# One visit instead of two: key sums of a whole batch in one slot, numerators of two head pairs in one slot, in blocks 2 to 6 of a fused attention and mixture-of-experts kernel

## The chip, the core and the metric

The kernel runs on one core of a Trainium2 chip. The core has five engines with instruction streams of their own: TensorE (PE, matrix products into the PSUM memory; its weight loads are listed as PEld), VectorE (DVE), ScalarE (ACT), GpSimd (POOL) and SyncE (SP). Here POOL and SP mainly issue DMA transfers. The metric is the device time of one launch in microseconds, the median of three runs.

## The reference

Linear attention with cosine and sine weights, then a layer of eight experts whose mixing weights are balanced by eight Sinkhorn rounds.

```python
q_p = phi(q, cos_w, sin_w)          # relu(q)*cos and relu(q)*sin side by side: 64 -> 128 features
k_p = phi(k, cos_w, sin_w)
kv  = einsum('bhsf,bhsd->bhfd', k_p, v)
z   = sum(k_p, axis=2)
num = einsum('bhsf,bhfd->bhsd', q_p, kv)
den = einsum('bhsf,bhf->bhs', q_p, z)[..., None] + 1e-06
x   = num / den                     # 8 batches, 8 heads, 576 tokens, 64 wide -> x is 4608 x 512
...
P = exp(x @ w_gate - max); 8 rounds of dividing P by its row sums and by its column sums
out = sum over the 8 experts e of P[:, e] * (relu(x @ w1[e]) @ w2[e])
```

## The kernel before

The kernel has two stages. In the first, the attention of one batch after another is laid in between the matrix products of expert 0. In the second, experts 1 to 7 run over all tokens. The change touches the first stage alone.

**Blocks and slots.** The first stage is a loop over blocks j = 0 to 6. A block is expert 0 over 512 tokens, in 16 slots. Slots 0 to 7 are the first product (ffn1): four matmuls of 512 columns into an h_ps bank, and a relu by ScalarE into hT. Slots 8 to 15 are the second product (ffn2): four matmuls of 512 columns into a y_ps bank, and after every second slot a copy by ScalarE into acc. After the matmuls of slot s of block j, the loop runs the functions that the table todo holds for (j, s); at(j, s, fn, ...) puts them there (lines 584 to 728). Functions of one slot run in the order in which at was called.

**Order.** TensorE, VectorE and ScalarE are reached through wrappers (te, ve, se) that tie each instruction to the one written before it on its engine. So the written order is the order in which each engine works, and an instruction that waits holds up all that is written behind it on its engine.

**What block j does besides expert 0.** For batch b = j + 1 it finishes the attention; for batch b + 1 it prepares; of batch b + 2 it loads the inputs. hk counts four head pairs, and a "half" is two of them. The functions are these:

- prep_k (line 339): the relu of a head pair's keys, on ScalarE for these blocks. prep_q (346): on VectorE, the relu and the multiplication with cosine and sine into q_p, one of three buffers; then SP issues a DMA that transposes q_p into one of eight q_pT places (two of them lie in acc_lo and acc_hi, and show under these names). prep_kv (371): on VectorE, the multiplication of the keys into k_p (four buffers) and the copy of the values beside a column of ones.
- sums (443): for one half, 2 head pairs x 9 chunks x 2 heads = 36 matmuls, each 64 rows by 128 columns of weights with 65 streamed columns. The two heads use the upper and the lower 64 rows of the array. The results go to two small_ps banks, from where ScalarE copies kv_sb and VectorE makes zsel.
- denominators (496): 24 matmuls with 32 columns of weights, side by side in three groups of columns; VectorE then adds the epsilon, takes the reciprocal, and splits it in two fp16 parts, hi and hl.
- attend (531), for one head pair: three matmuls of 96 rows and 192 streamed columns spread the reciprocals over the feature rows into two small_ps banks, ScalarE copies them to rb, then four matmuls of 128 rows and 64 columns of weights form the numerators (two of 384 and two of 192 streamed columns, the two heads in the left and the right 64 columns of the array) into two other banks, and VectorE multiplies them with rb into xT, which ffn1 and the gates read.
- gates (563): the logits of the tokens of batch j, and their exponential on ScalarE.
- load (198): six DMAs issued by POOL, held back until the VectorE instruction written just before it is done.

All small results, of sums, denominators, attend and gates, share one ring of four PSUM banks, named small_ps. A bank is used again when its readers are done.

**The slots before.** For j = 3 to 6: sums of the second half in slot 0, denominators in slot 3, gates in slot 5, attend in slots 6, 8, 10 and 12, prep_q in 4, 5, 7 and 9, prep_kv of the next batch in 7, 9, 11 and 13, loads in 11 and 12, and sums of the next batch's first half in slot 14. Block 2 differs from it in some of the prep slots. Block 6 prepares no further batch.

After block 6, two more blocks of expert 0 (j = 7 and 8) run beside the Sinkhorn rounds on VectorE. The rounds begin when gates(7), in slot 0 of block 7, have been exponentiated.

Of the kernel before, what the change touches and what calls it, by code (L numbers as in the profile page):

```python
# [25 lines left out]
def kernel(  # L26
# [19 lines left out]
    C = S // HP  # L46
# [134 lines left out]
    with ExitStack() as p1:  # L181
# [107 lines left out]
        C3 = C // 3  # L289
# [178 lines left out]
        def sums_made(b, half, kv_ps):  # L468
            kv_sb, zsel = kvs[b]
            W_ = D + 1 if b else D  # L470
            for hh in range(2):
                kv_v = kv_ps[hh][:, 0 : 2 * W_].rearrange("p (hk d) -> p hk d", d=W_)
                se.copy(out=kv_sb[:, 2 * half : 2 * half + 2, hh, :], in_=kv_v[:, :, 0:D])
                if b:
                    ve.tensor_tensor(
                        out=zsel[:, 4 * half + hh : 4 * half + 4 : 2, :],
                        in0=zmask[:, 4 * half + hh : 4 * half + 4 : 2, :],
                        in1=kv_v[:, :, D : D + 1].to_broadcast([P, 2, 32]),
                        op=ALU.mult,
                    )  # L480
# [47 lines left out]
            )  # L528
            hls[b] = hl

        def attend(b, hk):

            parts = ((0, 2 * C3), (2 * C3, C))
            rb_ps = [ps_s.tile([P, 512], FP32, name="small_ps") for _ in parts]
            rb = rb_pool.tile([P, C * HP], FP32, name="rb")
            for i, (c0, c1) in enumerate(parts):
                for j in range(c0 // C3, c1 // C3):
                    te.matmul(
                        out=rb_ps[i][:, (j * C3 - c0) * HP : ((j + 1) * C3 - c0) * HP],
                        lhsT=spread[0:96, j, hk].rearrange("p hh d -> p (hh d)"),  # L540
                        rhs=hls[b][:],
                        start=True,
                        stop=True,
                    )
                se.copy(out=rb[:, c0 * HP : c1 * HP], in_=rb_ps[i][:, 0 : (c1 - c0) * HP])
            num_ps = [ps_s.tile([P, 512], FP32, name="small_ps") for _ in parts]
            for i, (c0, c1) in enumerate(parts):
                for hh in range(2):
                    te.matmul(
                        out=num_ps[i][hh * HP : (hh + 1) * HP, 0 : (c1 - c0) * HP],  # L550
                        lhsT=kvs[b][0][:, hk, hh, :],
                        rhs=qTs[b, hk][:, c0:c1, hh * HP : (hh + 1) * HP],
                        start=True,
                        stop=True,
                    )
                ve.tensor_tensor(
                    out=xT[:, hk, b * S + c0 * HP : b * S + c1 * HP],
                    in0=num_ps[i][:, 0 : (c1 - c0) * HP],
                    in1=rb[:, c0 * HP : c1 * HP],
                    op=ALU.mult,  # L560
                )
# [25 lines left out]
        def at(block, slot, fn, *args):  # L587
            todo.setdefault((block, slot), []).append((fn, args))
# [40 lines left out]
        for hk in range(HK):  # L629
            attend(0, hk)  # L630
            for kt in ((), (0,), (1,), (2, 3))[hk]:
                for ft, h_ps in enumerate(first_ps):
                    te.matmul(
                        out=h_ps[:],
                        lhsT=w0[0][:, kt, ft * P : (ft + 1) * P],
                        rhs=xT[:, kt, 0:TCH],
                        start=(kt == 0),
                        stop=(kt == KT - 1),
                    )
                    if kt == KT - 1:  # L640
                        se.activation(out=hT[:, ft, 0:TCH], in_=h_ps[:], func=AF.Relu)
            for i in ((), (0,), (1, 2), ())[hk]:
                prep_k(1, i, i < 2)
            for i in ((), (0,), (1,), (2, 3))[hk]:
                if i == 3:
                    prep_k(1, i, False)
                prep_kp(1, i)
# [3 lines left out]
        for j in range(B):  # L651
            b = j + 1
            if j == 0:

                def sums_first(half):
                    sums_made(1, half, sums_begun(1, half))

                for hk in range(HK):
                    for i in range(3):
                        at(0, (5, 6, 6, 7)[hk], turn, 1, hk, i, i != 1)  # L660
                    if hk == 0:
                        at(0, 5, prep_q, 1, 3)
                    if hk == 2:
                        at(0, 6, prep_v, 1, 0, se.copy)
                        at(0, 6, prep_v, 1, 2, ve.tensor_copy)
                    if hk == 3:
                        at(0, 7, prep_v, 1, 1, se.copy)
                        at(0, 7, prep_v, 1, 3, ve.tensor_copy)
                for half in range(2):
                    at(0, 7, sums_first, half)  # L670
                at(0, 8, denominators, 1)
                at(0, 10, gates, 0)
                for hk in range(HK):
                    at(0, 11 + hk, attend, 1, hk)
            elif b < B:
                if j == 1:
                    at(0, 13, load, b + 1, 0, "q", True)
                    for hk in range(HK):
                        if hk >= 2:
                            at(j, 0, prep_k, b, hk, False)  # L680
                        at(j, 0, prep_kp, b, hk)
                        at(
                            j, (0, 0, 1, 3)[hk], prep_v, b, hk,
                            (ve.tensor_copy, se.copy)[hk // 2],
                        )
                    for name, half in (("q", 1), ("k", 0), ("k", 1), ("v", 0), ("v", 1)):
                        at(j, 0, load, b + 1, half, name, True)
                    at(j, 3, sums, b, 0)
                    at(j, 5, sums, b, 1)
                else:  # L690
                    at(j, 0, sums, b, 1)
                at(j, 6 if j == 1 else 3, denominators, b)
                for hk in range(HK):
                    at(j, (9, 10, 12, 13)[hk] if j == 1 else 6 + 2 * hk, attend, b, hk)
            if j:
                at(j, 5, gates, j)
            if j == 0:
                for half in range(2):
                    at(j, 3, load, b + 1, half)
                for slot, fn, hk, *args in (  # L700
                    (8, prep_q, 0), (11, prep_k, 0), (12, prep_q, 1), (12, prep_k, 1),
                    (13, prep_q, 2), (14, prep_q, 3),
                ):
                    at(j, slot, fn, b + 1, hk, *args)
            elif b + 1 < B:
                for slot, fn, hk in (
                    (4, prep_q, 0), (5, prep_q, 1), (8, prep_k, 0), (8, prep_q, 2),
                    (9, prep_k, 1), (10, prep_kv, 0), (10, prep_k, 2), (12, prep_q, 3),
                    (12, prep_kv, 1), (12, prep_k, 3), (13, prep_kv, 2), (14, prep_kp, 3),
                    (14, prep_v, 3),  # L710
                ) if j == 1 else (
                    (4, prep_q, 0), (5, prep_k, 0), (5, prep_q, 1), (6, prep_k, 1),
                    (7, prep_q, 2), (8, prep_kv, 0), (8, prep_k, 2), (9, prep_q, 3),
                    (10, prep_k, 3), (10, prep_kv, 1), (12, prep_kv, 2), (13, prep_kv, 3),
                ) if j == 2 else (
                    (3, prep_k, 0), (4, prep_q, 0), (4, prep_k, 1), (5, prep_q, 1),
                    (7, prep_kv, 0), (7, prep_k, 2), (7, prep_q, 2), (9, prep_q, 3),
                    (9, prep_k, 3), (9, prep_kv, 1), (11, prep_kv, 2), (13, prep_kv, 3),
                ):
                    at(j, slot, fn, b + 1, hk, *((se.copy,) if fn is prep_v else ()))  # L720
                at(j, 15 if j == 1 else 14, sums, b + 1, 0)
            if j == 1:
                for name in "qkv":
                    for half in range(2):
                        at(j, 12, load, b + 2, half, name, True)
            elif j and b + 2 < B:
                for half in range(2):
                    at(j, 11 + half, load, b + 2, half, "qkv", True)
# [524 lines left out]
```

The softmax here doesn't subtract the row's maximum and nothing guards it: scores larger than these inputs give would overflow.

## Time and profile before

| what | value |
|---|---|
| median of three runs | 982.71 us (981.52 to 983.88) |
| the profiled execution | 980.48 us, of it 978.8 us span |
| block 2 (67.9 to 87.6 us) | 19.70 us, TensorE busy 18.92 |
| blocks 3, 4, 5 (87.60 to 146.52 us) | 19.64 us each, TensorE busy 19.64 |
| block 6 (146.52 to 165.28 us) | 18.76 us, TensorE busy 18.76 |
| VectorE busy in blocks 3, 4, 5 | 14.10, 14.10 and 14.09 us of 19.64 |
| ScalarE busy in blocks 3, 4, 5 | 12.75, 12.74 and 12.75 us of 19.64 |

The costliest groups of small matmuls, from the page's list of groups (busy time in us, mean ns of one; then the idle time before them):

```profile
L109 PE MATMUL small_ps<-hl,acc_hi 96*128 96x192 f16 x96 | 13.3, 245 | 0.6 <-ACT rb L109 0.5
L109 PE MATMUL small_ps<-acc_lo,k_p 64*128 64x65 f16 x504 | 10.8, 191 | 1.1 <-ACT acc_lo L109 0.7 <-DVE acc_hi L109 0.3
L109 PE MATMUL small_ps<-q_pT,kv_sb 128*64 128x384 f16 (+1 forms) x96 | 10.7, 298 | 0.3
```

A row reads: line of the kernel (109 is the wrapper, so most rows have it), engine, operation, output <- inputs, the part of the array that is used (rows*columns), partitions x streamed columns and type, count. acc_lo and acc_hi stand for several small constants and buffers that lie in these tiles during the first stage: acc_lo here for the values with their column of ones, acc_hi for the spreading matrix. Matmuls overlap in the array, so a mean of 245 ns is a matmul's time from start to end, not its share of TensorE; that share is read from the distance of two starts.

### The profile page before, as it was taken

The numbers are of one execution on the slowest core, as the hardware profiler recorded it, in microseconds if no ns is written. First come the engines' busy times: TensorE is split into PE (matmuls) and PEld (weight loads), VectorE is DVE, ScalarE is ACT, GpSimd is POOL, SyncE is SP. The second block draws the span as 40 slices with busy tenths as digits, with TensorE's granted clock in tenths as the row PEclk, the third lists the DMA queues.
The fourth block names the chain that finished last, engine by engine and source line by source line (L and its number), as shares of the span: only waits on it lengthen the run. The fifth ranks groups of instructions, "written<-read, shape, count | busy, mean of one in ns | idle before, by whom it ended". The sixth has DMA issues, their size and how long they took to land.

```text
span 978.8 us, 20237 instructions
## 1 busy us (share of the span) xinstructions
PE 964.4 (99%) x7855; PEld 674.2 (69%) x7855; DVE 807.1 (82%) x1833; ACT 565.2 (58%) x1262; POOL 60.6 (6%) x82
## 2 busy tenths in 40 slices
PE   9999999999999999999999999999999999999997
PEld 6544454457777777777777777777777777777775
DVE  6767774888988888988888888988888888988887
ACT  5766665467776555555555555555555555555551
POOL 6231110010000000000000000000000000000001
PEclk9999999999999999999999999999999999999999
DMA  9999985330103401223103401223103401104435
GB/s 162 186 156 172 155 134 107 71 68 25 50 25 70 90 25 31 62 57 69 42 25 76 84 25 34 63 55 68 41 25 77 84 25 37 38 26 120 127 88 128
DMA packets 80336, 73.54 MB, mean 75 GB/s; under 512 B 33264, under 2 KB 72176, under 8 KB 80240
## 3 DMA queue, kind: packets, MB, share of 16 engines
q0 software_dynamic: 27232, 30.94, 20.3%
q1 hardware_dynamic: 52768, 41.06, 17.1%
q8 instruction: 61, 1.00, 0.4%
q14 instruction: 35, 0.29, 0.1%
q10 hardware_dynamic: 240, 0.26, 0.1%
HBM read 83.12 MB, written 12.98 MB: 98 GB/s over the span
## 4 chain that ended last, share of the span: by engine, by line
PE 88%; DMA 4%; DVE 3%; issue 2%; ACT 1%; POOL 1%; POOLq 0%; ACTq 0%; SPq 0%
PE rows_ps L109 33%; PE h_ps L109 26%; PE p_ps L109 11%; PE copied_ps L109 11%; PE y_ps L109 4%; PE small_ps L109 3%; DMA k_ld<-in_k_dram 1%; DMA w2e<-in_moe_w_dram 1%; DMA w1e<-in_moe_w_dram 1%; DMA acc_hi<-q_p 1%; DVE P_tok L109 1%; DVE colp L109 0%; POOL q_ld L202 0%; DVE rs L109 0%; DVE acc_hi L926 0%
## 5 line engine op out<-in xcount | busy, mean ns | idle before, releaser
L926 DVE SCALAR_TENSOR_TENSOR acc_lo<-rows_ps,P_tok,acc_lo 128x512 f32<-128x512 f32 (+1 forms) x322 | 203.5, 641 | 74.9 <-PE rows_ps L109 74.8
L109 PEld LDWEIGHTS <-H 128*128 128x128 f16 x2080 | 203.2, 98 | 82.5 <-issue 1.2
L862 ACT CAST u<-h_ps 128x384 f16<-128x384 f32 x288 | 137.8, 479 | 131.1 <-PE h_ps L109 131.1
L109 PEld LDWEIGHTS <-w1e 128*128 128x128 f16 x1632 | 157.3, 98 | 67.3 <-issue 5.7
L856 DVE CUSTOM_DVE_ANT_0 H<-p_ps,u 128x384 f16<-128x384 f32 x329 | 181.4, 551 | 6.4 <-PE p_ps L109 6.4
L109 PEld LDWEIGHTS <-hs 128*128 128x128 f16 x1500 | 146.6, 98 | 56.2
L109 PE MATMUL h_ps<-S,w1e 128*128 128x384 f16 x672 | 164.1, 326 | 0.7 <-ACT u L109 0.6
L109 PE MATMUL p_ps<-xT,T 128*128 128x384 f16 x672 | 164.1, 326 | 0.1
L109 PE MATMUL rows_ps<-V,H 128*128 128x256 f16 x1000 | 150.0, 273 | 0.7 <-DVE acc_hi L926 0.7
L109 PE MATMUL rows_ps<-w2e,hs 128*128 128x256 f16 x1000 | 150.0, 273 | 0.0
L109 PE MATMUL h_ps<-xT,w1e 128*128 128x384 f16 (+1 forms) x616 | 149.4, 350 | 0.1
L894 ACT ACTIVATE H<-h_ps 128x384 f16<-128x384 f32 x144 | 70.7, 491 | 95.0 <-PE h_ps L109 95.0
L109 PEld LDWEIGHTS <-T 128*128 128x128 f16 x1008 | 98.4, 98 | 29.9 <-issue 3.3
L109 PE MATMUL rows_ps<-w2e,H 128*128 128x256 f16 (+1 forms) x568 | 92.3, 285 | 0.0
L875 ACT COPY copied_ps<-h_ps 128x384 f32<-128x384 f32 x144 | 67.5, 469 | 35.1 <-PE h_ps L109 35.1
L885 ACT ACTIVATE H<-copied_ps 128x384 f16<-128x384 f32 x144 | 70.9, 493 | 20.3 <-PE copied_ps L109 20.3
L109 PE MATMUL h_ps<-S,T 128*128 128x384 f16 x336 | 81.8, 325 | 0.3 <-ACT copied_ps L109 0.3
L109 PE MATMUL copied_ps<-xT,w1e 128*128 128x384 f16 x336 | 82.1, 326 | 0.0
L109 PE MATMUL copied_ps<-w2e,H 128*128 128x256 f16 x504 | 75.5, 272 | 0.0
L109 PE MATMUL rows_ps<-V,hs 128*128 128x256 f16 x500 | 75.0, 272 | 0.0
L926 DVE SCALAR_TENSOR_TENSOR acc_lo<-copied_ps,P_tok,acc_lo 128x256 f32<-128x256 f32 x126 | 60.2, 478 | 0.4
L926 DVE SCALAR_TENSOR_TENSOR acc_hi<-rows_ps,P_tok,acc_hi 128x512 f32<-128x512 f32 (+1 forms) x56 | 41.3, 738 | 20.5 <-PE rows_ps L109 19.7
(145 smaller groups left out, 948.9 us busy)
## 6 DMA issues: line engine op xcount, KB each, us to landing
S<-x_saved SPq DMA_DIRECT2D x108, 192.0 KB, 2.4
out_dram<-acc_lo SPq DMA_DIRECT2D x62, 128.0 KB, 2.4
w1e<-in_moe_w_dram POOLq DMA_DIRECT2D x7, 1024.0 KB, 8.7
w2e<-in_moe_w_dram POOLq DMA_DIRECT2D x7, 1024.0 KB, 9.8
q_ld<-in_q_dram POOLq DMA_DIRECT2D x16, 288.0 KB, 6.5
k_ld<-in_k_dram POOLq DMA_DIRECT2D x16, 288.0 KB, 8.3
v_ld<-in_v_dram POOLq DMA_DIRECT2D x16, 288.0 KB, 9.3
x_saved<-S SPq DMA_DIRECT2D x18, 192.0 KB, 1.9
```

Of the source, the lines that this page charges most:

```text
L109: i = getattr(self.engine, name)(*args, **kwargs)
L856: latest = ve._custom_dve(TENSOR_ADD_SAT, out=out, in0=ps[:, 0:TU], in1=t[:], s0=FP32_MAX, s1=0.0)
L862: se.copy(out=t[:], in_=ps[:, 0:TU])
L875: se.copy(out=Y[:, 0:TU], in_=X[:, 0:TU])
L885: se.activation(out=h11, in_=Y[:, 0:TU], func=AF.Relu)
L894: se.activation(out=h12, in_=X[:, 0:TU], func=AF.Relu)
L926: ve.scalar_tensor_tensor(out=a, in0=rows, scalar=P_tok[:, g, self.e : self.e + 1], in1=a, op0=ALU.mult, op1=ALU.add,)
```

## The change

Two things are joined in blocks 2 to 6.

**Sums.** For j = 3 to 6 both halves of batch b are summed in slot 2 of block j. So block j - 1 no longer sums the first half in its slot 14, and it prepares only head pairs 0 and 1 of the next batch (prep_kv in slots 11 and 14); head pairs 2 and 3 follow in slots 0 and 1 of block j itself. The denominators move from slot 3 to slot 4. In block 2 the second half of batch 3 is still summed alone in slot 0, with the denominators in slot 3.

**Numerators.** attend is split in two: spread_out (three matmuls and the copies to rb) and numerators (four matmuls and the products into xT). In blocks 2 to 6 spread_out of the four head pairs runs in slots 7, 8, 10 and 11; the numerators of head pairs 0 and 1 run together in slot 9, those of 2 and 3 in slot 13. Blocks 0 and 1 call both parts one after the other, as before.

prep_q moves to slots 5, 6, 8 and 10 (in block 2: 4, 5, 8 and 10).

```diff
-        def attend(b, hk):
-
-            parts = ((0, 2 * C3), (2 * C3, C))
+        parts = ((0, 2 * C3), (2 * C3, C))
+        rbs = {}
+
+        def attend(b, *hks):
+            for hk in hks:
+                spread_out(b, hk)
+            for hk in hks:
+                numerators(b, hk)
+
+        def numerators_of(b, *hks):
+            for hk in hks:
+                numerators(b, hk)
+
+        def spread_out(b, hk):
+
             rb_ps = [ps_s.tile([P, 512], FP32, name="small_ps") for _ in parts]
...
                 se.copy(out=rb[:, c0 * HP : c1 * HP], in_=rb_ps[i][:, 0 : (c1 - c0) * HP])
+            rbs[b, hk] = rb
+
+        def numerators(b, hk):
+
+            rb = rbs.pop((b, hk))
             num_ps = [ps_s.tile([P, 512], FP32, name="small_ps") for _ in parts]
...
+                elif j == 2:
+                    at(j, 0, sums, b, 1)
                 else:
-                    at(j, 0, sums, b, 1)
-                at(j, 6 if j == 1 else 3, denominators, b)
+                    at(j, 0, prep_kv, b, 2)
+                    at(j, 1, prep_kv, b, 3)
+                    at(j, 2, sums, b, 0)
+                    at(j, 2, sums, b, 1)
+                at(j, 6 if j == 1 else 3 if j == 2 else 4, denominators, b)
                 for hk in range(HK):
-                    at(j, (9, 10, 12, 13)[hk] if j == 1 else 6 + 2 * hk, attend, b, hk)
+                    if j == 1:
+                        at(j, (9, 10, 12, 13)[hk], attend, b, hk)
+                    else:
+                        at(j, (7, 8, 10, 11)[hk], spread_out, b, hk)
+                if j > 1:
+                    at(j, 9, numerators_of, b, 0, 1)
+                    at(j, 13, numerators_of, b, 2, 3)
...
                     (4, prep_q, 0), (5, prep_k, 0), (5, prep_q, 1), (6, prep_k, 1),
-                    (7, prep_q, 2), (8, prep_kv, 0), (8, prep_k, 2), (9, prep_q, 3),
-                    (10, prep_k, 3), (10, prep_kv, 1), (12, prep_kv, 2), (13, prep_kv, 3),
+                    (8, prep_q, 2), (8, prep_k, 2), (10, prep_q, 3), (10, prep_k, 3),
+                    (11, prep_kv, 0), (14, prep_kv, 1),
                 ) if j == 2 else (
-                    (3, prep_k, 0), (4, prep_q, 0), (4, prep_k, 1), (5, prep_q, 1),
-                    (7, prep_kv, 0), (7, prep_k, 2), (7, prep_q, 2), (9, prep_q, 3),
-                    (9, prep_k, 3), (9, prep_kv, 1), (11, prep_kv, 2), (13, prep_kv, 3),
+                    (3, prep_k, 0), (4, prep_k, 1), (5, prep_q, 0), (6, prep_q, 1),
+                    (7, prep_k, 2), (8, prep_q, 2), (10, prep_q, 3), (10, prep_k, 3),
+                    (11, prep_kv, 0), (14, prep_kv, 1),
                 ):
                     at(j, slot, fn, b + 1, hk, *((se.copy,) if fn is prep_v else ()))
-                at(j, 15 if j == 1 else 14, sums, b + 1, 0)
+                if j == 1:
+                    at(j, 15, sums, b + 1, 0)
```

## The prediction

> **What bounds the kernel now.** I read the page first: busy shares, then the granted clock.
>
> ```profile
> PE 964.4 (99%) x7855; PEld 674.2 (69%) x7855; DVE 807.1 (82%) x1833; ACT 565.2 (58%) x1262; POOL 60.6 (6%) x82
> ...
> PEclk9999999999999999999999999999999999999999
> ```
>
> TensorE has no slack on the whole, at full clock. The change lies in blocks 2 to 6, from 67 to 165 us, so next the waits of TensorE in 68 to 166 us. There is one:
>
> ```profile
> PE small_ps L109 <- DMA acc_hi<-q_p: 0.8, 1, 0.8
> ```
>
> It is in slot 3 of block 2 (72.7 us), for a transposed query prepared in block 1, which is not edited; I keep it. Elsewhere in these blocks only fewer TensorE nanoseconds can help. Are there any to be had? The chain of waits here holds TensorE alone (start us, us):
>
> ```profile
> 103.76 1.83 PE y_ps L109 x8
> 105.60 0.68 PE small_ps L109 x36
> 106.27 0.97 PE y_ps L109 x4
> 107.24 0.86 PE h_ps L109 x4
> 108.11 0.68 PE small_ps L109 x36
> ```
>
> The same four 512-column matmuls take 0.86 us after their own kind and 0.97 us after the 36 small matmuls of a half of the sums. So 0.11 us is paid on the way out, and something perhaps on the way in. The timeline of TensorE shows the starts around two calls of attend (start, us from first start to last end):
>
> ```profile
> 115.18 0.41 PE L109 MATMUL small_ps<-hl,acc_hi 96*128 96x192 f16 x3
> 115.53 0.44 PE L109 MATMUL small_ps<-q_pT,kv_sb 128*64 128x384 f16 x4
> 115.89 1.04 PE L109 MATMUL h_ps<-xT,w1e 128*128 128x512 f16 x4
> 116.77 1.03 PE L109 MATMUL y_ps<-w2e,hT 128*128 128x512 f16 x4
> 117.63 0.41 PE L109 MATMUL small_ps<-hl,acc_hi 96*128 96x192 f16 x3
> 117.97 0.44 PE L109 MATMUL small_ps<-q_pT,kv_sb 128*64 128x384 f16 x4
> 118.34 1.47 PE L109 MATMUL y_ps<-w2e,hT 128*128 128x512 f16 x6
> ```
>
> **Numerators.** From start to start 512 columns take 216 ns (0.86 / 4), so 192 take 81 ns. Three spreading matmuls should take 243 ns; the next group starts after 345. The numerators are two column tiles side by side (128*64), in time 384 + 192 columns, 243 ns; the next full matmul starts 0.36 to 0.37 us later. The single records put the excess at four places: 94 ns between the last 192-column spread and the first numerator, 25 ns in the first numerator, 98 ns after the last, 11 ns in the next full matmul. That is 228 ns for a visit to this tile shape. In front of the spreading there is nothing: it starts 216 ns after the full matmul before it, and its first interval is only 6 ns longer than 81.
>
> Before, each of four head pairs pays 228 ns. After, two visits carry two pairs each; the second pair's four matmuls stand in the shape already, at 160 + 80 ns. Saved: 2 x 228 ns a block, in 5 blocks: 10 x 0.228 = 2.28 us. Against it stands one thing that the trace lacks: **the spreading (96*128) is now followed by a full matmul**, 20 times. Bounds: 0 to 98 ns each (the exit of the other shapes), so 0 to 1.96 us. The nearest row is its own entry, 6 ns. The Trainium skill ("TensorEngine Tiling (Array Packing)", Tiling Modes) says that a change of tiling mode drains TensorE, and lists modes of 128, 64 or 32 rows, none of 96. Read strictly, 96 rows run in the 128-row mode and the exit is free; read as any change of shape, 98 ns. By the first I save 2.28 us, by the second 0.32. The free entry decides for the first; I take 5 ns, 0.1 us in all. Numerators: **2.18 us**.
>
> **Sums.** Entry: the last full matmul before 105.53 started 312 ns earlier instead of 216, so 96. Exit: 124 ns from the last pair's start, instead of 32, so 92; then 11 in the full matmul. With 5 ns of a slower start: 204 ns for a visit. Two halves without anything between occur in this trace, in block 0:
>
> ```profile
> 33.13 1.03 PE L109 MATMUL small_ps<-acc_lo,k_p 64*128 64x65 f16 x54 [0.74 <-ACT acc_lo L109]
> 34.10 1.04 PE L109 MATMUL y_ps<-w2e,hT 128*128 128x512 f16 x4
> ```
>
> 54 in 0.97 us including the exit, against 0.68 for 36: 18 more cost 0.29, 16 ns each, with no break at the halves. Batches 4 to 7 are merged (batch 3 keeps two visits): 4 x 0.204 = **0.82 us**. One half moves from block j-1 to block j; that sums to nothing. Denominators and gates keep their number.
>
> **Do other engines now make TensorE wait?** I laid the new block beside the old rows. Zero is the end of slot 7, where the first spreading starts. For TensorE: slot 8 ends at 1.12, second spreading to 1.38, slot 9 to 2.24, numerators 0 and 1 2.34 to 2.95, slot 10 to 3.81, third spreading, slot 11, fourth spreading to 5.18, slot 13 to 6.9, numerators 2 and 3 to 7.6, block end 9.3. For VectorE the durations are these (overlapping starts count):
>
> ```profile
> 112.30 0.35 DVE L109 TENSOR_SCALAR den<-small_ps 96x192 f32<-96x192 f32 x1 [2.79 <-PE small_ps L109]
> 112.69 1.35 DVE L109 RECIPROCAL den<-den 96x192 f32<-96x192 f32 x1
> ...
> 114.36 0.41 DVE L109 SCALAR_TENSOR_TENSOR hl<-hi,lo,den 96x192 f16<-96x192 f16 x1
> ...
> 116.72 0.82 DVE L109 TENSOR_TENSOR xT<-small_ps,rb 128x384 f16<-128x384 f32 x2
> 117.45 0.75 DVE L109 TENSOR_TENSOR k_p<-k_ld,acc_hi 128x1152 f16<-128x1152 f16 x1
> ```
>
> The reciprocals: denominators to first spreading is again three slots and the gates; hl is done at 114.77 and used at 115.18, so 0.41 us stay. Queries 0, 1 and 2 (1.02 us each, start to start: 114.69, 115.70, 116.72) fill VectorE to 2.54; the numerators' products take 0.73 a pair, to 3.4 and 4.15. Here a rule of the skill speaks against the change (same page, Performance Considerations, PSUM Bottleneck): tiling speeds up TensorE but not the evacuation of PSUM. Merged, four banks are filled in 0.6 us and emptied in 1.46, and small_ps has four. By the rule, the third spreading waits for a bank. By the rows: it needs its banks at 3.81, they are free at 3.4 plus some 0.1; the fourth needs its at 4.9, free at 4.2. On ScalarE the copies of the second spreading stand behind prep_k 2 (0.58) and end at 2.28 and 2.57, for numerators that want the banks at 2.60 and 2.76. No wait, but covers of 0.2 to 0.3 us only. If they fail I expect no more than 0.3 us a block; I count nothing.
>
> At the block's end: products 2 and 3 end at 8.75, the next block's first full matmul on hk 2 comes at 9.76: cover 1.0 (2 us before). Then prep_kv 1, 2 and 3 at 1.03 each end at 9.8, 10.8 and 11.85; the merged sums start at 12.0 and reach hk 3 at 12.9: cover 1.0. If VectorE is later than that, TensorE waits at slot 2.
>
> Queues: SP's transposes go out at slots 5, 6, 8 and 10 instead of 4, 5, 7 and 9. The fourth q_p needs the first's buffer (three of them) 3.8 us after its issue; landing takes 3.3 us in most rows. They are wanted 10 us later. POOL's six loads of 288 KB are released by the first v copy, not the third, in relation to the block about 1.7 us earlier; their first reader, prep_k 0 of the next block, keeps slot 3, so its cover grows. The load of expert 1's weights (147.28 us) may now be held to slot 1 or 2 of block 6 by the later reading of k and v: about the same moment, first used at 173.84. After block 6 everything hangs on gates(7), VectorE having waited 2.98 us there; the saving is passed on whole.
>
> **Sum.** 2.18 + 0.82 = **3.0 us**. The profiled execution, 978.8 span and 980.48 with what lies around it, becomes 975.8 and 977.5. It is 2.2 below the median of the runs; the difference carries over: 982.7 - 3.0 = **979.7 us**.
>
> **Rivals.** (a) The exit of the spreading costs a full change: 0.32 + 0.82 = 1.1 us, 981.6. For it: three other shapes pay about 95 on both sides; against it the free entry. 0.1. (b) Banks or copies come late: 0.3 us in five blocks gives back 1.5, 981.2. For it the thin covers, against it the rows. 0.12. (c) **Slower**: prep_q's transpose is the mechanism. If its landing takes over 4 us, q_p 3 waits in VectorE's queue, and behind it numerators 2 and 3, prep_kv 1, 2 and 3, and so slots 0 and 2 of the next block. The landing of 6.6 us in block 1, beside loads, would cost 0.5 us a block by the covers above; from about 7.5 us, 1.3 us in four blocks, 5.2 in all, the kernel ends 2 us slower, at 985. Against it: nothing in blocks 3 to 6 landed later than 4.2 us. 0.04. The written order is kept by dependencies, so that the change doesn't happen I leave out. My forecast: 0.74.
>
> **Numbers.** A measurement here tells 0.2%, 2.0 us, from no change. The forecast's 3.0 lies over it, by about the scatter of the runs (981.52 to 983.88): of 0.74, some 0.68 show as faster; of (b) and (a) some 0.06. Faster 0.74, same 0.21, slower 0.05. The range from 978.2 (no exit cost, lucky runs) to 981.8 takes in (a) and (b).
>
> **What would show it.** Blocks 3 to 6 last 19.64, 19.64, 19.64 and 18.76; I expect 19.0 for the first three and 18.9 for the last (18.5 for block 2, now 19.70), and gates(7) 3.0 us earlier. Sums x72 should last 1.26 with one exit. The interval from the last spread to the next full matmul should be about 85 ns; 180 shows (a). Waits of TensorE for ACT rb or DVE xT at slots 9 to 10 show (b); waits for k_p at slot 2 or xT at slot 0 show (c). If the blocks shrink and the end doesn't move, the sinkhorn stage swallowed it and I am wrong there.

## The result and the profile after

| | before | after |
|---|---|---|
| first comparison, median of four runs each | 982.12 us (981.47 to 983.88) | 978.03 us (977.90 to 978.92) |
| ratio, 95% interval | | 0.9958 (0.9940 to 0.9975) |
| the profiled execution, and its span | 980.48, 978.8 us | 978.92, 977.2 us |
| blocks 3, 4, 5 | 19.64, 19.64, 19.64 us | 19.03, 18.93, 19.03 us |
| block 6 | 18.76 us | 18.93 us |

The kernel is faster, by 4.1 us (0.4%) in this comparison. The forecast was 3.0 us less, 979.7 us with a range from 978.2 to 981.8; the measured time lies just below it. The two profiled executions differ by only 1.6 us. So three numbers have to be brought together: 4.1, 3.0 and 1.6.

The chain of waits of the changed kernel in block 4 (start us, us, what) answers to the chain that the prediction read:

```profile
106.53 2.63 PE h_ps L109 x12
109.16 1.25 PE small_ps L109 x72
110.42 1.83 PE h_ps L109 x8
...
116.12 0.25 PE small_ps L109 x3
116.37 0.86 PE y_ps L109 x4
117.23 0.25 PE small_ps L109 x3
117.48 0.86 PE y_ps L109 x4
118.34 0.61 PE small_ps L109 x8
118.96 0.97 PE y_ps L109 x4
```

The 72 matmuls of both halves take 1.25 us in one visit, where two visits took 0.68 each and 0.11 more after each. The spreading takes 0.25 us, which is the 243 ns that its 576 columns need, and the four full matmuls after it take 0.86 us, as after their own kind. In the single records a full matmul starts 81 or 82 ns after the last spreading one, which is the time of its 192 columns. So **leaving the 96-row shape is free**, the one cost that the trace of before couldn't show. After the numerators a group of four still takes 0.97.

Block 4 holds 16 gate matmuls (0.38 us), blocks 3 and 5 hold 20 (0.48 us); so block 4 is now 0.10 us shorter than they are. Before, it was not. There its last visit took 0.71 us where the others took 0.61, as the chain of waits of before shows:

```profile
120.24 0.61 PE small_ps L109 x7
...
122.69 0.71 PE small_ps L109 x7
```

The timeline of VectorE in before has the products of the third head pair just ahead of it:

```profile
122.26 0.81 DVE L109 TENSOR_TENSOR xT<-small_ps,rb 128x384 f16<-128x384 f32 x2
```

In the single records the second pair of the numerators of this visit starts at 123.13 us, 257 ns after the first instead of 183, and 0.06 us after these products end; they read the PSUM bank that comes round to it in the ring of four. So the kernel before had a wait of 0.10 us in block 4 that the list of waits doesn't show and the prediction passed over. The change removes it.

The covers came out as laid beside the old rows. In the timeline of VectorE of the changed kernel for block 4, hl is done at 115.54 us, 0.4 us before the first spreading starts (115.95). With zero at 116.12, the products of head pairs 0 and 1 start at 2.62 us and end at 4.17 (predicted 4.15):

```profile
115.13 0.41 DVE L109 SCALAR_TENSOR_TENSOR hl<-hi,lo,den 96x192 f16<-96x192 f16 x1
...
117.82 0.76 DVE L109 TENSOR_TENSOR q_p<-q_ld,acc_hi 128x1152 f16<-128x1152 f16 x1
118.74 1.55 DVE L109 TENSOR_TENSOR xT<-small_ps,rb 128x384 f16<-128x384 f32 x4 [0.16 <-PE small_ps L109]
```

What differs between the two executions lies outside the merged slots. The waits of TensorE in the changed kernel, from 64 to 166 us (total us, times, longest):

```profile
PE small_ps L109 <- DMA acc_hi<-q_p: 1.0, 1, 1.0
...
PE small_ps L109 <- DVE acc_lo L109: 0.3, 1, 0.3
...
PE small_ps L109 <- DVE k_p L109: 0.2, 1, 0.2
```

All three are in slots 0 and 3 of block 2, before the first merged visit. They are waits for what blocks 0 and 1 loaded and prepared, which the change leaves alone. The profile of before had only the first, with 0.8; a second profile of before (e1 below) has all three. The changed kernel also entered block 1 0.4 us later (45.55 against 45.17 us). From the last denominators of block 2, which end this wait, to the first matmul of block 7, before takes 72.72 to 165.12 us, 92.40, and after 73.81 to 163.26, 89.45: **2.95 us less**, for 3.0 predicted. So the profile carries the count, and the rest of the 4.1 has to be explained by something else.

### The profile page after: what moved, and what is told of

The parts are those of the page before. It is cut to its first block, busy times and chain, and to the rows that moved or that the text cites. A ratio compares the mean times of both kernels' runs of the same rounds, so it can differ in the third digit from the quotient of the medians.

```text
span 977.2 us, 20236 instructions
## 1 busy us (share of the span) xinstructions
PE 962.4 (98%) x7855; PEld 675.7 (69%) x7855; DVE 807.8 (83%) x1833; ACT 564.7 (58%) x1262; POOL 60.6 (6%) x82
## 4 chain that ended last, share of the span: by engine, by line
PE 88%; DMA 4%; DVE 3%; issue 2%; ACT 1%; POOL 1%; POOLq 0%; ACTq 0%; SPq 0%
PE rows_ps L109 33%; PE h_ps L109 26%; PE p_ps L109 11%; PE copied_ps L109 11%; PE y_ps L109 4%; PE small_ps L109 2%; DMA k_ld<-in_k_dram 1%; DMA w1e<-in_moe_w_dram 1%; DMA w2e<-in_moe_w_dram 1%; DMA acc_hi<-q_p 1%; DVE P_tok L109 1%; DVE colp L109 0%; POOL q_ld L202 0%; DVE rs L109 0%; DVE acc_hi L955 0%
```

## The experiments

Theory A: the visits to another tile shape account for the change, and what goes beyond 3.0 us in the first comparison is scatter that arises before block 2's denominators. Theory B: most executions of the kernel before lose a further microsecond in blocks 2 to 6, which its profile happened not to show. The last column is the time from the last denominators of block 2 to block 7. The runs e1 to e4, e5 to e8, and e9 and e10 were made on three chips; between these groups only the ratios can be compared.

| run | ratio to before (95% interval) | median, us | blocks 3, 4, 5, 6, us | stage, us |
|---|---|---|---|---|
| e1 before again | 1.0001 (0.9992 to 1.0009) | 980.82 | 19.64, 19.63, 19.67, 18.76 | 92.41 |
| e2 after again | 0.9973 (0.9966 to 0.9980) | 978.79 | 19.03, 18.93, 19.03, 18.93 | 89.42 |
| e3 sums alone | 0.9998 (0.9990 to 1.0006) | 980.93 | 19.48, 19.38, 19.48, 19.38 | 91.71 |
| e4 numerators alone | 0.9984 (0.9975 to 0.9993) | 979.94 | 19.19, 19.09, 19.19, 18.31 | 90.44 |
| e5 split, not merged | single run | 980.98 | 19.48, 19.38, 19.48, 19.38 | 92.26 |
| e6 four at once | single run | 984.43 | 19.98, 19.88, 20.32, 19.88 | 95.35 |
| e7 block 2 too | 0.9959 (0.9944 to 0.9975) | 978.43 | 19.03, 18.93, 19.03, 18.93 | |
| e8 after, third time | 0.9967 (0.9955 to 0.9979) | 978.90 | 19.03, 18.93, 19.03, 18.93 | 89.41 |
| e9 loads later | 0.9960 (0.9947 to 0.9973) | 977.79 | 19.03, 18.93, 19.03, 18.93 | |
| e10 both | 0.9963 (0.9954 to 0.9973) | 977.19 | 19.03, 18.93, 19.03, 18.93 | |

The kernel before, run beside them, had medians of 981.3 us (54 runs, e1 to e4), 981.92 (20 runs, e5 to e8) and 980.83 (25 runs, e9 and e10).

**e1, the kernel before once more, unchanged.**

> The kernel before once more, with a profile of its own. Theory A (only the visits to another tile shape count: 3.0 us from the count, the rest of the measured 4.1 is scatter of the stage before block 2): blocks 3 to 6 again last 19.64, 19.64, 19.64 and 18.76 us, and TensorE waits only at the start and once in slot 3 of block 2; the ratio to the kernel before is 1 within 0.1%. Theory B (before, most executions lose a further 1 us or more in blocks 2 to 6, by late loads of k or q, which the profiled execution happened not to show): a block of 3 to 6 is longer than 19.64, with a wait of ScalarE's prep_k or of TensorE in it.

Its blocks repeat to 0.03 us. In blocks 3 to 6 the last visit of block 4 again lasts 0.09 us longer than the others, and that of block 5 0.02; nothing else waits there. ScalarE waited once for keys (0.7 us) without costing TensorE anything. That is as A has it; B, which needs a microsecond, finds no support in this second profile.

**e2, the changed kernel once more, unchanged.**

> The changed kernel once more. Theory A: 3.0 us less than the kernel before, ratio 0.9969; blocks 3 to 6 last 19.0, 18.9, 19.0 and 18.9 us, and what changes from one profile to the next lies before slot 4 of block 2. Theory B: 4 us less, ratio 0.9958, in a close interval.

Sixteen runs give 0.9973, which is 2.6 us of 981.3 (2.0 to 3.3): the 4.1 of the first comparison is not repeated. Blocks 3 to 6 are the same to 0.01 us. But the waits before them are not, in the same program:

```profile
PE small_ps L109 <- DMA acc_hi<-q_p: 2.6, 1, 2.6
PE small_ps L109 <- ACT rb L109: 1.3, 1, 1.3
```

The first row is again the transposed query of slot 3 in block 2; it cost 1.0 us in one execution of this program and 2.6 in the other. The second is in block 1 (59.9 us), where the profiles vary as well. B falls; A stands. Next, e3 and e4 try the two parts of the change one at a time.

**e3, the sums alone.**

```diff
                     else:
-                        at(j, (7, 8, 10, 11)[hk], spread_out, b, hk)
-                if j > 1:
-                    at(j, 9, numerators_of, b, 0, 1)
-                    at(j, 13, numerators_of, b, 2, 3)
+                        at(j, 7 + 2 * hk, attend, b, hk)
```

> The sums as in the changed kernel, attend whole for each head pair, in slots 7, 9, 11 and 13. Theory A: 4 merged visits at 0.204 us, 0.8 us less than before, ratio 0.9992; blocks 3, 4 and 5 last 19.44. Theory B (the moved prep steps and loads bring the rest): about 1.8 us less, ratio 0.998.

The stage is 0.70 us shorter, for 0.82 expected; the ratio's interval holds anything from 1.0 us less to 0.6 more. Of the 0.70, 0.10 is the wait of block 4, which is gone here too, and 0.07 was lost to a wait in block 2. A merged visit by itself (block 3) gives 0.16 instead of 0.204. The missing 0.05 is a small wait that the merged kernels have and before has not. In the chain of the changed kernel above the twelve matmuls of slots 0 to 2 take 2.63 us instead of the 2.59 of 12 x 216 ns; in the single records the first matmul of slot 2 comes 263 ns after its predecessor. It needs the h_ps bank that the relu of slot 0 empties, and that relu ends at 108.09 us, 50 ns before the matmul starts at 108.14. The relu isn't held up by other work: ScalarE sat idle for 0.34 us before it, until slot 0's matmuls were done. The one slot in between is too short a cover. Before, a half of the sums lay between slots 0 and 1 and covered this. That this bank is what the matmul waits for is read from these times, not tested.

**e4, the numerators alone.** The sums as before, spreading in slots 6, 7, 9 and 10, and prep_kv of head pairs 0 to 2 in slots 8, 10 and 12, one slot later than before. Beside the changed kernel the numerators move so:

```diff
-                    at(j, 9, numerators_of, b, 0, 1)
-                    at(j, 13, numerators_of, b, 2, 3)
+                    at(j, 8, numerators_of, b, 0, 1)
+                    at(j, 12, numerators_of, b, 2, 3)
```

> Spreading in slots 6, 7, 9 and 10, numerators of two head pairs in slots 8 and 12, sums and their prep as before (the first prep_kv after the products). Theory A: 10 merged visits at 0.228 us, 2.2 us less than before, ratio 0.9978; blocks 3, 4 and 5 last 19.2. Theory B: the gap to 4.1 is missing here, as the loads are as before: ratio 0.9978 as well, and e2 less e3 and e4 leaves about 1 us.

Blocks 3 to 6 are 0.45 to 0.55 us shorter, as counted. Block 2 gained little (14.64 us from its denominators to block 3, before 14.72), and the chain of waits shows why:

```profile
77.75 0.61 ACT hT L109
78.36 0.38 ACT rb L109
...
78.78 0.50 PE small_ps L109 x4
```

In this layout prep_k stands between ScalarE's copies, so that the bank of the second spreading came free late and the second pair of numerators started 365 ns after the one before, instead of 80. This is rival (b) of the prediction, in an arrangement one slot tighter than the change. The visit took 1.08 us instead of 0.71. Without this loss of 0.37 us, e4 would save 2.33 us. With the 0.70 of e3 that makes 3.03, for 2.95 of the whole change; the 0.10 of block 4 stands in both parts. So to about 0.1 us the two parts are the whole.

**e5, split but not merged.**

```diff
-                    at(j, 9, numerators_of, b, 0, 1)
-                    at(j, 13, numerators_of, b, 2, 3)
+                    for hk in range(HK):
+                        at(j, (8, 9, 12, 13)[hk], numerators, b, hk)
```

> The changed kernel with its split, but numerators of one head pair in a slot, in slots 8, 9, 12 and 13: four visits a block as in e3. Theory A (the visits alone): blocks 3 to 6 last as in e3, 19.48, 19.38, 19.48 and 19.38 us, within 0.05. Theory C (the split itself helps, since the products no longer wait for the copies of the spreading): shorter than 19.4 where e3 has 19.48.

Its blocks equal those of e3 to 0.01 us. Pulling spreading and numerators apart brings nothing; joining two visits does. Theory C falls. The chain shows a lone visit of a head pair and a lone spreading side by side:

```profile
100.11 0.37 PE small_ps L109 x4
100.48 0.97 PE y_ps L109 x4
101.45 0.25 PE small_ps L109 x3
101.70 0.86 PE y_ps L109 x4
```

Only the visit to the narrow columns is followed by the longer group. (In block 2 this kernel waited 0.5 us for a copy to rb, as e4 did.)

**e6, all four numerators in one slot.**

```diff
-                    at(j, 9, numerators_of, b, 0, 1)
-                    at(j, 13, numerators_of, b, 2, 3)
+                    at(j, 12, numerators_of, b, 0, 1, 2, 3)
```

> The changed kernel with the numerators of all four head pairs together in slot 12: one visit a block. Theory A alone: 0.228 us less in each block, 18.80 and 18.70. Rule of the PSUM banks (eight results, four banks, emptied at 0.73 us a pair): the third pair waits for the first pair's products and the fourth for the second's, about 0.8 us in all, so that a block lasts 19.5 to 19.7, with TensorE waiting for DVE xT in slot 12.

The blocks are 0.95 us longer than the changed kernel's in three cases and 1.29 in one, although a visit fewer is paid: 0.228 us are saved and about 1.2 lost. The estimate of 0.8 was too small, the mechanism as expected. The waits of TensorE show it, ten times in five blocks:

```profile
PE small_ps L109 <- DVE xT L109: 3.4, 10, 0.7
```

The results of four pairs need eight banks where there are four, and VectorE empties those of a pair in 0.73 us. Two pairs in a visit are as many as the ring holds. In the one longer block VectorE came to the products 0.3 us later than in the block before, as its fourth query had waited 1.8 us for a transposition instead of 1.3: the path that rival (c) names.

**e7, block 2 like the others.** Both halves of batch 3 in slot 2 of block 2, none in block 1, denominators in slot 4:

```diff
-                elif j == 2:
-                    at(j, 0, sums, b, 1)
                 else:
-                    at(j, 0, prep_kv, b, 2)
-                    at(j, 1, prep_kv, b, 3)
+                    if j > 2:
+                        at(j, 0, prep_kv, b, 2)
+                        at(j, 1, prep_kv, b, 3)
                     at(j, 2, sums, b, 0)
...
-                if j == 1:
-                    at(j, 15, sums, b + 1, 0)
```

> The changed kernel with block 2 like the later ones: both halves of batch 3 summed in slot 2 of block 2 (none in slot 15 of block 1), denominators in slot 4. Theory A: one visit less, 0.2 us, and the wait for the transposed query (0.8, 1.0 and 2.6 us in the profiles) is covered by a slot and the sums, 1.2 us: 0.8 to 1.2 us less than the changed kernel, ratio to the kernel before about 0.9962. Rival: the late transposed query is bound to the loads at the start, so that the wait only moves: no more than 0.2 us.

In its profile the wait for the transposed query is still 0.7 us, as TensorE arrives earlier. Its median is 0.5 us below that of e8, between the 0.8 to 1.2 of theory A and the 0.2 of the rival, and the intervals of the two overlap: not decided.

**e8, the changed kernel a third time, beside e7.**

> The changed kernel on the same chip as e7, to compare the two. Theory A: ratio to the kernel before 0.9973, as in e2; in its profile the stage from the denominators of block 2 to block 7 lasts 89.4 us again, and [...]0.28 us near 676 us again, if it depends on the program and not on chance.

The stage lasts 89.41 us again, and the wait for the transposed query was 2.4 us this time. The expected 0.28 us near 676 us is there as well. It was found by laying the starts of the last 6,000 matmuls of each trace beside those of before: after and e2 keep their distance to 0.03 us from 240 us on, except for one jump at this place. The timeline of TensorE and its weight loads in the changed kernel shows it:

```profile
675.47 0.49 PE L109 MATMUL p_ps<-xT,T 128*128 128x384 f16 x2
...
676.08 0.48 PE L109 MATMUL h_ps<-S,T 128*128 128x384 f16 x2
676.09 0.10 PEld L109 LDWEIGHTS <-T 128*128 128x128 f16 x1 [0.35 <-issue]
```

The starts of the two groups of matmuls lie 0.61 us apart; in before, the same two lie 0.33 us apart. Of the gap, 0.35 us counts as "issue": the weight load waited for nothing that the profile shows. The jump is in after, e2, e3, e5, e6, e7 and e8, at the same matmul each time, and not in before, e1, e4, e9 and e10. All executions of one program agree, the three of the changed kernel and the two of before; so it seems to depend on the program and not on chance. The old order of the sums isn't what avoids it, since e9 and e10 have the new one. The fetch of instructions is an obvious suspect, but a packet of 16 KB on a queue that the page calls "instruction" arrives 0.5 to 1.2 us ahead of this matmul in all twelve traces, with the jump and without it. The cause stays open.

**e9 and e10, the scatter before block 2.** In block 1 the loads of k and v of batch 4 go out three slots later, and block 2 uses the keys later; e10 has e7's change as well.

```diff
-                        at(j, 12, load, b + 2, half, name, True)
+                        at(j, 12 if name == "q" else 15, load, b + 2, half, name, True)
...
-                    (4, prep_q, 0), (5, prep_k, 0), (5, prep_q, 1), (6, prep_k, 1),
-                    (8, prep_q, 2), (8, prep_k, 2), (10, prep_q, 3), (10, prep_k, 3),
-                    (11, prep_kv, 0), (14, prep_kv, 1),
+                    (5, prep_q, 0), (6, prep_q, 1), (8, prep_q, 2), (9, prep_k, 0),
+                    (10, prep_q, 3), (11, prep_kv, 0), (12, prep_k, 1), (13, prep_k, 2),
+                    (14, prep_kv, 1), (14, prep_k, 3),
```

> The changed kernel; in block 1 the loads of k and v of batch 4 go out in slot 15 instead of 12, and block 2 uses the keys later. Theory (the scatter before block 2, which made the first comparison show 4.1 us, comes from the last transposed query landing beside these loads, in 6.2 to 8.5 us): it lands in 3.3 to 5 us, TensorE's wait in slot 3 of block 2 goes, 0.8 to 2 us less than the changed kernel, and blocks 3 to 6 last as before. Rival (the query itself is late because of the loads of block 0): landing and wait stay.

> e7 and e9 together: block 2 like the later ones, loads of k and v in slot 15. Theory: no wait of TensorE in block 2 and one visit less, 1 to 2 us less than the changed kernel, ratio to the kernel before 0.995 to 0.996, the best of all. Rival: the waits of block 2 are replaced by waits for the late keys or for the copies of the spreading, no better than e7.

The last transposed query, issued near 66 us, took this long to land, in the lists of transfers of e8 and then of e9 (median us at the end of the row):

```profile
acc_hi<-q_p SPq DMA_TRANSPOSE x1, 8.1
```

```profile
acc_hi<-q_p SPq DMA_TRANSPOSE x1, 5.4
```

Over the ten profiles with the old loads it took 6.2 to 8.5 us, in e9 5.4 and in e10 6.3. So the landing missed the 3.3 to 5 us of the theory in both, and in e10 it is no shorter than in the best profile with the old loads: that these loads make it late isn't shown. In e9 TensorE no longer waits for it, as expected; in e10 the wait is 0.2 us. From its first matmul to that of block 3, block 2 lasts 18.48 us in e9, 20.67 in before and 20.28 in the changed kernel. (This isn't the 18.5 of the prediction, though the numbers agree. The 19.70 of before, from which that was counted, begins at 67.9 us, 1.1 us after the block's first matmul at 66.77, and it holds the wait of 0.8, which e9 hasn't.) In e9 a wait of 1.1 us in block 1 remains, for a copy to rb. The medians are 977.79 and 977.19 us beside 980.83 for before on the same chip. The intervals of their ratios, 0.9960 and 0.9963, overlap with those of the changed kernel, which wasn't run beside them, and 0.28 us of any lead is the jump near 676 us that they happen not to have. So e10 may be the best version, by something under 1 us, and that isn't shown. Why the landing varies between executions of one program stays open.

## Why the prediction was right or wrong

**What failed is the last step, "the difference carries over: 982.7 - 3.0 = 979.7 us"**, and the lower end of the range built on it. The mechanism was right; the base was mis-sized. It was the median of three runs, 982.71 us. In 99 later runs beside e1 to e10 the kernel before had medians of 980.83 to 981.92 us; 3.0 less than these is 977.8 to 978.9, which holds the measured 978.03. The prediction saw that the page's 980.48 us lay 2.2 us below its base, and still left only 1.5 us below the forecast, from 979.7 to 978.2. (For the profiled execution it said 977.5 us. That one took 978.92: 1.09 us more were lost before the last denominators of block 2, and 0.28 at 676 us.)

The other side of the comparison scattered too. Four runs of the changed kernel gave 978.03 us, 16 and 12 later ones 978.79 and 978.90, which lie inside the range. So the 4.1 us of the first comparison are some 0.8 us of a high base and some 0.8 us of a low draw, as far as runs on several chips can be compared, beside the true difference. That the time fell just outside the range, and not just inside, is chance; that the range was so narrow on this side is the error. The ratios of the 16 and 12 runs, 0.9973 and 0.9967, are 2.6 and 3.2 us; the count from the traces is 2.95 - 0.28 = 2.67. Where the scatter comes from is shown in part: waits in blocks 1 and 2 for loads, for copies and for the last transposed query, 0.3 to 2.6 us at one place, differ between executions of one program.

**Numerators, 2.18 us: right.** e3 and the changed kernel differ in nothing else in blocks 3 to 6: 0.45 us a block, for 0.44 counted. The unknown of this term, the exit of the spreading, was 0. Of the two readings of the list of modes in the Trainium skill ("TensorEngine Tiling (Array Packing)", Tiling Modes), the strict one fits these traces, and rival (a) falls.

**Sums, 0.82 us: 0.65 measured**, 0.16 us a block in four blocks. The term that was put at nothing is the wait of slot 2 for the relu of slot 0, 0.05 us a block; the prediction searched the covers of the merged visits alone.

**The sum of 3.0 is met by 2.95 with some luck.** The shortfall of the sums is made up in part by the 0.10 us of block 4, a wait that the prediction took for work.

**Covers: right.** TensorE doesn't wait for a bank, a copy, k_p or xT at the places named for rivals (b) and (c), but for 0.03 us once, in slot 9 of block 2. The covers are as thin as said: in block 2 of e4 and e5, one slot less cost 0.4 to 0.6 us. e6 shows what the Trainium skill says of PSUM (same page, PSUM Bottleneck), that tiling speeds up TensorE but not the emptying of PSUM, at 1.2 us a block.

**"After block 6 everything hangs on gates(7); the saving is passed on whole": not quite.** Through the Sinkhorn rounds it is, to 0.01 us. In the second stage the program of the changed kernel loses 0.28 us at 676 us, for a cause that stays open.

## What to carry to other kernels

Where TensorE is the bound, count its visits to other tile shapes and not the small matmuls: a visit cost 0.20 to 0.23 us here, with one half or two, one head pair or two in it, so gather the small work that can be ready together. The ring of PSUM banks sets the limit: two pairs filled the four banks and won, four pairs lost five times what they saved. And a forecast of 0.3% needs a base known to better than that; take a difference from stages of the trace, and leave room in the range for the scatter of the base and of the few runs it will be measured by.

## What the runs showed of the hardware that was not expected

A change of tile shape cost about 95 ns on the way in and 92 to 98 on the way out, for the 64-row and the 64-column matmuls alike, but a 96-row matmul next to 128-row ones cost nothing on either side (it starts 216 ns after a full one, and the next full one 81 or 82 ns after the last of it). TensorE can lose 0.28 us at a matmul while it waits for nothing that the profile shows, 500 us behind the part that was changed: in after, e2, e3, e5, e6, e7 and e8, and in none of before, e1, e4, e9 and e10. A transposing DMA of 288 KB landed in 3.2 to 3.4 us in most rows; the one issued near 66 us, when six loads of the same size go out, took 6.2 to 8.5 in ten profiles.
